# The seventh of nine token groups takes its second product from seven products of quarters; the weight sums move earlier and wholly to GpSimd

## The chip, the cores and the metric

One core of one Trainium2 chip runs the kernel. The metric is the device time of one execution in microseconds (us). Engines: TensorE (PE, matmuls; PEld its weight loads), VectorE (DVE), ScalarE (ACT), GpSimd (POOL), SyncE (SP, whose queue issues most DMAs).

## The reference

Windowed causal attention for 8 batches, 8 heads, 576 positions, head size 64, and behind it an MLP with SiLU for the 4608 rows of 512 that it gives:

```python
scores = scale * np.matmul(q, k.transpose(0, 1, 3, 2))
mask = (rel >= 0) & (rel < window)                 # window 128
scores = np.where(mask, scores + bias[None], -1000000000.0)
attn = np.exp(scores - np.max(scores, axis=-1, keepdims=True))
attn = attn / (np.sum(attn, axis=-1, keepdims=True) + 1e-09)
attn_out = np.matmul(attn, v).astype(np.float32)   # -> x, 4608 x 512
h = x @ w_in                                       # w_in 512 x 2048
g = h * (1.0 / (1.0 + np.exp(-h)))
return (g @ w_out).astype(np.float32)              # w_out 2048 x 512
```

## The kernel before

**Tiles and stages.** The 4608 rows are nine groups of 512, g = 0 to 8. For a group the 2048 columns of w_in are 16 blocks f; n = 16g + f counts them all. From group 2 on each float32 operand is a pair of float16 numbers, high part and remainder, and a product is three matmuls: high x high, high x remainder, remainder x high. `gemm1` makes h for one n in PSUM, `act1` takes tanh on ACT, `act2` makes h(1 + tanh) on DVE, `act3` rounds to `gh` on ACT, `act4` takes the remainder `gl` on DVE, and `gemm2` multiplies by w_out into four PSUM banks w, x, y, z, which collect over the group; `store` empties them.

**Groups in FAST** (7 and 8) do this otherwise. In them an n is a pair (t, j): 256 of the group's rows and two f blocks, j and j + 8, which makes a product of 2 x 2 quarters. `act_sums` forms sums of the quarters of g, so `act3` and `act4` work on seven blocks of 128 columns, and `gemm2_fast` uses 7 products of quarters (M1 to M7) where 8 would be plain: 21 matmuls of 256 columns. `join_products` and `add_corners` bring them together behind the last j of each t. The sums of w_out's quarters that this needs are made once, on POOL and ACT (`sum_float`, `sum_make`, `sum_hi`, `sum_lo`, for j = 0 to 7), and kept in SBUF. Group 8 (SEVEN) also makes h from 7 products; the sums of w_in for it (`in_float` to `in_lo`) are made in groups 2 to 4, stored to DRAM (`in_away`) and read back (`in_back`).

**Attention** is 72 pairs p (a tile of 128 rows, four of the heads). For each: `scores` on PE into the two PSUM banks "a" (L495), `row_max` on DVE (L526), `exps` on ACT, `p_hi` on ACT (L551), the remainder `p_lo` on POOL from pair 18 on (L557, helper line), two transposing DMAs on SP (`hl`, L567), `attend` on PE (`av`, L609), `normalize`, `x_hi`, `x_lo`. `lo16` (L443) and `v_lo` (L476) are remainders on DVE. The bank for `av` is again one of "a". `vscale_finish` makes a batch's scales, its last stage by a small matmul (L325) into a bank "a".

**What sets the order.** Nothing is scheduled by the machine: a table `plan` says at which position each function is issued, and every engine takes its instructions in the order of issue. A group has 64 positions, four for an n: two halves of `gemm1`, two of `gemm2`. Group 6 is 384 to 447. Pair p has its scores at `at(p)`, nine pairs to a group, 7 positions apart, in groups 1 to 6. `gemm2` of an n stands behind `gemm1` of a later one: one later in groups 0 to 6 (with none left over at a group's end), three later in group 7 (LAG), four in group 8.

```python
SUMS, SUMS_STEP = 302, 17
IN_SUMS = (186, 200, 214, 228, 242, 256, 270, 284)
FAST = (NG - 2, NG - 1)
left = LAG + (n >= SEVEN * NF - 1) if g in FAST else 1
```

## Time and profile before

| | |
|---|---|
| median of 3 runs | 901.03 us (900.76 to 901.49) |
| the profiled execution | 901.33 us |
| its span, first to last instruction | 899.5 us |
| busy: PE, PEld | 891.8 us (99%), 592.2 us (66%) |
| busy: DVE, ACT, POOL | 611.3, 613.3, 411.5 us |

The profile is of one execution. Its span leaves out some 1.8 us that lie around the instructions. Busy times add up over the whole span; what an engine's work is worth must be read from the stretch in which it lies. PE's sequence through a group is best seen in the chain of waits, which merges equal matmuls that follow each other.

### The profile page before, as it was taken

Reading aid. Unit: us, or ns where it says so; the run is one execution under the profiler, and the core shown is the slowest. Engines: PE = TensorE matmul, PEld = TensorE weight load, DVE = VectorE, ACT = ScalarE, POOL = GpSimd, SP = SyncE. Lnnn points to the kernel's source line nnn. Section 1 sums busy time; section 2 is a strip of 40 time slices with the busy share of each in tenths; the row PEclk is TensorE's granted clock in tenths of the full one; section 3 lists DMA queues with packets and bytes.
Section 4 is the critical chain, followed back from the end, with each engine's and each line's share of the span. In section 5 each row is a group of like instructions: output and inputs, shape, how many; then the busy total and the mean of one; then the engine's idle time right before and its main releaser. Section 6 shows DMA issues by size and latency. Waiting matters only on the chain. (4 is left out here: it accounts for less than half of the span.)

```text
span 899.5 us, 20129 instructions
## 1 busy us (share of the span) xinstructions
PE 891.8 (99%) x7657; PEld 592.2 (66%) x7657; DVE 611.3 (68%) x1591; ACT 613.3 (68%) x1336; POOL 411.5 (46%) x462
## 2 busy tenths in 40 slices
...
GB/s 301 402 204 230 274 56 134 71 94 95 106 205 224 204 95 89 228 175 212 142 176 118 129 106 147 89 96 81 135 145 85 60 107 162 85 37 7 20 26 24
DMA packets 206160, 120.98 MB, mean 134 GB/s; under 512 B 170864, under 2 KB 173040, under 8 KB 206064
## 3 DMA queue, kind: packets, MB, share of 16 engines
...
## 5 line engine op out<-in xcount | busy, mean ns | idle before, releaser
L1130 PE MATMUL o<-w,gh 128*128 128x512 f16 (+1 forms) x896 | 273.6, 387 | 0.1
L920 PE MATMUL h<-xt,w 128*128 128x512 f16 (+1 forms) x1344 | 269.7, 349 | 0.0
L557 POOL TENSOR_TENSOR hr<-t,hr 128x512 f16<-128x512 f32 (+1 forms) x108 | 119.7, 1121 | 253.3 <-ACT hr L551 170.7
L920 PEld LDWEIGHTS <-w 128*128 128x128 f16 x1344 | 126.3, 98 | 112.3 <-issue 3.3
L961 DVE SCALAR_TENSOR_TENSOR h<-gt,h 128x512 f32<-128x512 f32 x112 | 77.8, 694 | 159.9 <-ACT gt L955 159.6
L1130 PE MATMUL o<-w,gl 128*128 128x512 f16 (+1 forms) x448 | 172.0, 384 | 0.2
L955 ACT ACTIVATE gt<-h,tsc 128x512 f32<-128x512 f32 x112 | 76.3, 681 | 92.9 <-PE h L920 79.5
L1130 PEld LDWEIGHTS <-gh 128*128 128x128 f16 x640 | 59.3, 98 | 66.7
L526 DVE CUSTOM_DVE_ANT_0 t<-sp,tab 128x256 f32<-128x256 f32 (+1 forms) x288 | 99.9, 401 | 1.9 <-PE sp L502 1.3
L551 ACT ACTIVATE hr<-t 128x512 f16<-128x512 f32 (+1 forms) x128 | 74.1, 598 | 2.6 <-DMA hl<-hr 2.6
L541 ACT ACTIVATE t<-t,mx,vsc 128x256 f32<-128x256 f32 (+1 forms) x144 | 74.8, 578 | 1.2
L1007 DVE SCALAR_TENSOR_TENSOR gl<-h,gh 128x512 f16<-128x512 f32 x80 | 55.0, 687 | 24.2 <-ACT gh L993 23.8
L541 ACT ACTIVATE t<-t,mx 128x256 f32<-128x256 f32 (+1 forms) x144 | 61.8, 488 | 4.5 <-DVE mx L526 3.8
L993 ACT ACTIVATE gh<-h 128x512 f16<-128x512 f32 x80 | 47.2, 590 | 22.4 <-DVE h L961 22.1
L609 PEld LDWEIGHTS <-hl 128*128 128x128 f16 x1464 | 52.0, 98 | 15.8 <-issue 4.5
L171 POOL TENSOR_TENSOR x<-xs,x 128x256 f16<-128x256 f32 x54 | 39.1, 725 | 43.5 <-ACT x L648 43.3
L609 PE MATMUL av<-v,hl 128*128 128x65 f16 (+1 forms) x1464 | 55.4, 193 | 0.9 <-DVE mx L526 0.6
L1130 PEld LDWEIGHTS <-gl 128*128 128x128 f16 x320 | 31.3, 98 | 37.9 <-DVE gl L1007 0.3
L1130 PEld LDWEIGHTS o<-w,gh 128*128 128x128 f32 x256 | 45.6, 188 | 10.0 <-issue 0.5
L925 PE MATMUL h<-xh,w 128*128 128x512 f32 x128 | 44.5, 404 | 0.0
L892 PE MATMUL h<-xt,w 128*128 128x256 f16 x384 | 44.2, 273 | 0.0
L171 POOL TENSOR_TENSOR w<-wm,w 128x512 fp32r<-128x512 f32 x32 | 43.0, 1343 | 2.6
...
## 6 DMA issues: line engine op xcount, KB each, us to landing
...
```

The source lines that it names most:

```text
L171: engine.tensor_sub(out, a, b)
L526: nc.vector.tensor_tensor_reduce(out=st[p]["t"][u][:, h, 2 * P - n :], in0=st[p]["sp"][h][:, u, o].rearrange("p o c -> p (o c)"), in1=tab[ ...
L541: nc.scalar.activation(x, x, AF.Exp, bias=mx[:, 2 * u + h : 2 * u + h + 1], scale=scale)
L551: nc.scalar.activation(split_of(p, u, hr)[:, 0], t[:, :, 2 * P - n :], AF.Copy, scale=scale)
L557: nc.gpsimd.tensor_sub(hr[:, 1], t[:, :, 2 * P - n :], hr[:, 0])
L609: nc.tensor.matmul(av[:, 2 * u + h, : rhs.shape[-1]], lhs, rhs, start=(n == 0), stop=(n == len(seq) - 1), skip_group_check=True,)
L920: nc.tensor.matmul(o, w[:, wp, cc], x, start=start and k == 0, stop=stop, skip_group_check=True)
L955: nc.scalar.activation(gt, hps[n], AF.Tanh, scale=scale)
L961: nc.vector.scalar_tensor_tensor(out=h, in0=gt, scalar=1.0, in1=h, op0=ALU.add, op1=ALU.mult)
L993: nc.scalar.activation(gh, gt, AF.Copy, scale=cut_of(n))
L1007: nc.vector.scalar_tensor_tensor(out=gl, in0=gt, scalar=cut_of(n), in1=f32(gh) if n // NF < OUT16 else gh, op0=ALU.mult, op1=ALU.subtract)
L1130: nc.tensor.matmul(ops[ti], a[:, t], w, start=(f == 0 and i == 0), stop=(f == NF - 1 and i == len(seq) - 1), skip_group_check=True,)
```

## The change

Group 6 joins FAST: `gemm1` there runs by `gemm1_fast` (24 matmuls of 256 columns for 12 of 512), `gemm2` from seven products. Its `act_sums` run on POOL; group 7's (ALONE) stay on DVE. Since attention still runs in group 6, its products use banks w, x, y, z for both t. The lag grows from one to three within group 5 (`lag_of`), and the boundary from 5 to 6 and from 6 to 7 no longer works its n off to the end.

The sums of w_out are needed a group earlier: they start at position 178 (before 302) and take turns with those of w_in, 24 positions to a j for both. The copies that ACT made for them go to POOL (`copy_hi`), and w_in's quarters are formed in place. `away` is stored 7 positions behind the start of a w_in sum. Of each pair's two `p_lo`, that of u = 1 goes from POOL to DVE (LOW_DVE). The last batch's scales are finished at 268, 274, 281, 288, and several offsets of attention move by one to three positions.

```diff
--- before.py
+++ after.py
@@ -63,7 +63,7 @@
 OWN = ("w1_12", "w1_13")
 OWN_FIRST = ("w0_15", "w0_14")
 FREE = ("w1_14", "w0_15", "w0_14", "w1_12", "w0_13")
-FINISH = {1: (37, 42, 45), 2: (166, 168, 169, 170), 3: (268, 271, 273, 275)}
+FINISH = {1: (37, 42, 45), 2: (166, 168, 169, 170), 3: (268, 274, 281, 288)}
 BOUNDS = {2: (125, 4), 3: (195, 6)}
 LOAD1, REDUCE1 = (-9, -8, -6, -5, -4), (25, 21, 17, 13, 11)
 RAW16 = ("w1_0", "w1_1")
@@ -71,19 +71,37 @@
 PACKED = ("w1_4", "w1_5", "w1_6")
 LESS = 2
 CUT = 2.0 ** (LESS - 20)
-IN_TAGS = {0: "w1_2", 1: "w1_3", 2: "w1_0", 4: "w1_5"}
-IN_SUMS = (186, 200, 214, 228, 242, 256, 270, 284)
-IN_BACK = {2: 440, 3: 444, 4: 460, 5: 468, 6: 474, 7: 480}
-AWAY = ("w1_7", "w1_8")
+IN_TAGS = {0: ("w1_2", 1), 1: ("w1_3", 1), 2: ("w1_0", 1), 3: ("q", 2), 4: ("w1_5", 1), 5: ("x", 4), 6: ("x", 4)}
+SUMS, SUMS_STEP = 178, 24
+IN_GAP = 17
+HI_SUM, HI_IN = 1, 1
+IN_SUMS = tuple(SUMS + SUMS_STEP * j + IN_GAP for j in range(8))
+IN_AWAY = 7
+IN_BACK = {2: 462, 3: 484, 4: 470, 5: 490, 6: 494, 7: 480}
 X_TAGS = ("w1_1", "w1_4")
-X_SUMS = (450, 453, 456, 459, 462, 465, 468, 472, 471, 476, 474, 478, 479, 487, 481, 489)
+X_SHIFT = 4
+ALONE_POOL = 0
+ALONE_LATE = 6
+X_SUMS = tuple(X_SHIFT + n for n in (450, 453, 456, 459, 462, 465, 468, 472, 471, 476, 474, 478, 479, 487, 481, 489))
 NB = 2
-FAST = (NG - 2, NG - 1)
+FAST = (NG - 3, NG - 2, NG - 1)
+ALONE = NG - 2
 SEVEN = NG - 1
 HALF_F = NF // 2
 LAG = 3
-SUMS, SUMS_STEP = 302, 17
-OUT_TAGS = {3: ("w1_14", "w1_9"), 4: ("w1_13", "w1_14"), 6: ("w1_5", "w1_6")}
+RAMP = (4, 9)
+ACT_LATE = 6
+ACT_LOW = 2
+V_HI, V_LO = 8, 4
+IN_HI16, IN_LO16 = (9, 8), (6, 4)
+ATTEND = 11
+EXPS = (2, 3)
+P_HI = (3, 3)
+P_LO = (4, 5)
+X_OFF = 2
+LOW_DVE = 1
+X_DVE = 0
+OUT_TAGS = {3: ("q", 2), 4: ("q", 2), 5: ("q", 2)}
 SUM_TAGS = tuple(f"w1_{k}" for k in range(7, 15))
 MORE_TAGS = (("w1_15", 1), ("k", KSLOTS), ("k", KSLOTS))
 STATS, CONV_IN, CONV_OUT = 68, 55, 108
...
         hr = split_of(p, u, st[p]["hr", u])
         if p >= LOW_POOL:
-            nc.gpsimd.tensor_sub(hr[:, 1], t[:, :, 2 * P - n :], hr[:, 0])
+            minus(nc.vector if u and LOW_DVE else nc.gpsimd, hr[:, 1], t[:, :, 2 * P - n :], hr[:, 0])
             return
         nc.vector.scalar_tensor_tensor(
             out=hr[:, 1], in0=t[:, :, 2 * P - n :], scalar=PSCALE, in1=hr[:, 0], op0=ALU.mult, op1=ALU.subtract
...
             cols = slice(q * 4 * D, (q + 1) * 4 * D)
-            minus(nc.gpsimd if p >= LOW_POOL else nc.vector, xt[i][:, 1, cols], st[p]["x"], xt[i][:, 0, cols])
+            minus(nc.gpsimd if p >= LOW_POOL and not X_DVE else nc.vector, xt[i][:, 1, cols], st[p]["x"], xt[i][:, 0, cols])
             if q == 1:
...
 
+    def copy_hi(on_pool, out16, a):
+        if on_pool:
+            nc.gpsimd.tensor_copy(out16, a)
+        else:
+            nc.scalar.copy(out16, a)
+
     def sum_hi(j, k):
...
-        piece["q"] = [both[1][:, s].rearrange("p (s c) -> p s c", s=2) for s in range(2)]
-        w = pool.tile([P, 2, 4, DM // 2], F16, tag=IN_TAGS[j] if j < 2 else AWAY[j % 2], bufs=1, name=f"wx{j}")
+    def in_tile(j):
+        tag, bufs = IN_TAGS[j] if j < 2 else ("big", 2)
+        w = pool.tile([P, 2, 4, DM // 2], F16, tag=tag, bufs=bufs, name=f"wx{j}")
         win[j] = [w[:, part] for part in range(2)]
 
...
     def in_float(j, k):
         if k == 0:
-            in_pieces(j)
+            piece["room"] = pool.tile([P, 2, DM], F32, tag="big", name=f"wb{j}")
+        piece[k] = piece["room"][:, k]
+        r = piece[k]
         w = w16[0, j + k * HALF_F]
-        nc.gpsimd.tensor_add(piece["r"][k].rearrange("p (c f) -> p c f", c=NCC), w[:, 0], w[:, 1])
+        nc.gpsimd.tensor_add(r.rearrange("p (c f) -> p c f", c=NCC), w[:, 0], w[:, 1])
...
     def in_make(j, k):
-        (a11, a12), (a21, a22) = ([r[:, h * DM // 2 : (h + 1) * DM // 2] for h in range(2)] for r in piece["r"])
-        one, two = piece["q"]
+        (a11, a12), (a21, a22) = ([piece[k][:, h * DM // 2 : (h + 1) * DM // 2] for h in range(2)] for k in range(2))
         if k == 0:
-            nc.gpsimd.tensor_add(one[:, 0], a21, a22)
-            nc.gpsimd.tensor_sub(one[:, 1], one[:, 0], a11)
-        else:
-            nc.gpsimd.tensor_sub(two[:, 0], a11, a21)
-            nc.gpsimd.tensor_sub(two[:, 1], a12, one[:, 1])
+            nc.gpsimd.tensor_add(a22, a21, a22)
+            nc.gpsimd.tensor_sub(a21, a11, a21)
+        else:
+            nc.gpsimd.tensor_sub(a11, a22, a11)
+            nc.gpsimd.tensor_sub(a12, a12, a11)
...
     IN_WORK = (
-        [(in_float, 0)], [(in_float, 1)], [(in_make, 0)], [], [(in_make, 1)], [], [(in_hi, 0)], [(in_lo, 0)],
-        [(in_hi, 1)], [(in_lo, 1)],
+        [(in_float, 0)], [(in_float, 1)], [(in_make, 0)], [(in_make, 1), (in_hi, 1)], [(in_lo, 1), (in_hi, 0)], [],
+        [(in_lo, 0)],
     )
...
     def act_sums(n):
         if n == LAST:
             return
-        engine, a = nc.gpsimd if n // NF == SEVEN else nc.vector, gact[n]
+        engine, a = nc.vector if n // NF == ALONE and n % NF >= ALONE_POOL else nc.gpsimd, gact[n]
         pairs = a[:, 0:4].rearrange("p (a b) c -> p a b c", b=2)
...
         dt = F32R if n // NF < OUT16 else F16
-        gh = pool.tile([P, TG], dt, tag="gh", name=f"gh{n}")
-        gl = pool.tile([P, TG], dt, tag="gl", name=f"gl{n}")
+        if n // NF < OUT16:
+            gh, gl = (pool.tile([P, TG], dt, tag=tag, name=f"{tag}{n}") for tag in ("gh", "gl"))
+        else:
+            both = pool.tile([P, 2, TG], dt, tag=("gh", "gl")[n % 2], name=f"gb{n}")
+            gh, gl = both[:, 0], both[:, 1]
         if n // NF < IN16:
             (nc.vector.tensor_copy if at_edge(n) else nc.scalar.copy)(gh, gt)
         elif n // NF < OUT16 and at_edge(n):
...
         products, first = (M5, M2, M1, M3, M4, M7, M6), 4
-        if j == 0 and g == SEVEN:
+        if j == 0 and g != ALONE:
             first = 3
         elif j == 0 and t:
             products = (M3, M4, M5, M2, M1, M7, M6)
...
                 if j == 0 and side == 0 and a is gh:
-                    ops[b] = psum.tile([P, DM], F32, tag=("axaz" if t or g == SEVEN else "wxyz")[b], bufs=2 if (t or g == SEVEN) and b % 2 == 0 else 1, name=f"m{g}_{t}_{b}")
+                    free = g == SEVEN or g == ALONE and t
+                    tag = ("axaz" if free else "wxyz")[b]
+                    ops[b] = psum.tile([P, DM], F32, tag=tag, bufs=2 if tag == "a" else 1, name=f"m{g}_{t}_{b}")
                 for part in parts:
                     nc.tensor.matmul(
                         product(k), a[:, k], sum_part(k, j, part),
...
         if half == 0:
-            both = pool.tile([P, 2, 2, DM // 2], F32, tag="w1_6", bufs=1, name=f"of{g}_{t}")
-            st["out"] = [both[:, k] for k in range(2)]
-            st["once"] = once = pool.tile([P, 2, DM // 2], F32, tag="rv", bufs=2, name=f"once{g}_{t}")
-            nc.scalar.activation(once.rearrange("p a c -> p (a c)"), ops[1], AF.Copy, scale=scale)
+            if g < ALONE:
+                st["out"] = [pool.tile([P, 2, DM // 2], F32, tag="q", bufs=2, name=f"of{g}_{t}_{k}") for k in range(2)]
+            else:
+                both = pool.tile([P, 2, 2, DM // 2], F32, tag="w1_6", bufs=1, name=f"of{g}_{t}")
+                st["out"] = [both[:, k] for k in range(2)]
+            once = st["out"][1]
+            nc.scalar.activation(once, ops[1].rearrange("p (a c) -> p a c", a=2), AF.Copy, scale=scale)
             for k in range(2):
                 nc.vector.scalar_tensor_tensor(
                     out=st["out"][0][:, k], in0=product(M1), scalar=scale, in1=once[:, k], op0=ALU.mult, op1=ALU.subtract
                 )
             return
-        (corner, other), once = st["out"], st["once"]
+        corner, other = st["out"]
         nc.vector.scalar_tensor_tensor(
-            out=other, in0=ops[0].rearrange("p (a c) -> p a c", a=2), scalar=scale, in1=once, op0=ALU.mult, op1=ALU.add
+            out=other, in0=ops[0].rearrange("p (a c) -> p a c", a=2), scalar=scale, in1=other, op0=ALU.mult, op1=ALU.add
         )
...
     def store(g, ti):
         tag, bufs = ("x", 4) if ti > 1 else ("io", 2)
         if ti > 1 and g > 2:
-            tag, bufs = (OUT_TAGS[g][ti % 2], 1) if g in OUT_TAGS else ("big", 2)
+            tag, bufs = OUT_TAGS[g]
         ot = pool.tile([P, DM], F32, tag=tag, bufs=bufs, name=f"ot{g}_{ti}")
...
     SUM_WORK = (
-        [(sum_float, 0)], [(sum_float, 1)], [(sum_make, 0)], [(sum_make, 1)], [(sum_make, 2), (sum_hi, 0)],
-        [(sum_hi, 1), (sum_lo, 0)], [(sum_hi, 2)], [(sum_lo, 1)], [(sum_lo, 2)],
+        [(sum_float, 0)], [], [(sum_float, 1)], [], [(sum_make, 0)], [], [(sum_make, 1), (sum_hi, 0)], [],
+        [(sum_make, 2), (sum_hi, 1)], [(sum_lo, 0), (sum_hi, 2)], [], [(sum_lo, 1)], [], [(sum_lo, 2)],
     )
...
         put(n + 1, row_max, p, 1)
-        put(2 if p == 2 * GT else n + 2, exps, p, 0)
-        put(2 if p == 2 * GT else n + 3, exps, p, 1)
+        plain = p < LOW_POOL
+        put(2 if p == 2 * GT else n + (2 if plain else EXPS[0]), exps, p, 0)
+        put(2 if p == 2 * GT else n + (3 if plain else EXPS[1]), exps, p, 1)
...
+        elif not plain:
+            for u in range(2):
+                put(n + P_HI[u], p_hi, p, u)
+                put(n + P_LO[u], p_lo, p, u)
+                put(n + P_LO[u], p_transpose, p, u)
...
-                put(a - (7 if i < 2 * GT else 5), v_hi, i)
-                put(a - (3 if i == 2 * GT else 4), v_lo, i)
+                put(a - (7 if i < 2 * GT else V_HI), v_hi, i)
+                put(a - (3 if i == 2 * GT else 4 if i < 2 * GT else V_LO), v_lo, i)
...
         if j > 1:
-            put(IN_SUMS[j] + 17, in_away, j)
+            put(IN_SUMS[j] + IN_AWAY, in_away, j)
             put(IN_BACK[j], in_back, j)
...
+        def lag_of(n):
+            g, f = divmod(n, NF)
+            if n == NG * NF - 1 or f == NF - 1 and g + 1 < FAST[0]:
+                return 0
+            if g in FAST:
+                return LAG + (n >= SEVEN * NF - 1)
+            return 1 + (f >= RAMP[0]) + (f >= RAMP[1]) if g + 1 in FAST else 1
...
-                left = LAG + (n >= SEVEN * NF - 1) if g in FAST else 1
-                if f == NF - 1 and (g not in FAST or g == NG - 1):
-                    left = 0
+                left = lag_of(n)
...
+                        if n % NF == NF - 1 and g not in FAST and g + 1 not in FAST:
                             turn_over(n)
                         else:
-                            late = 1 if n == 0 else 9 if n == SEVEN * NF - 1 else 11 if n == SEVEN * NF - 2 else 4 if g in FAST and n % NF > 1 else 2
-                            ahead(late + 1 + (late == 4) if n % NF else late, act4, n)
+                            late = 1 if n == 0 else 9 if n == SEVEN * NF - 1 else 11 if n == SEVEN * NF - 2 else ALONE_LATE if g in FAST and n % NF > 1 else 2
+                            if g in FAST and g < ALONE:
+                                late = ACT_LATE
+                            ahead(late + (ACT_LOW if g in FAST and g < ALONE else 1) + (late == ALONE_LATE and g >= ALONE) if n % NF or g in FAST else late, act4, n)
                             ahead(late, act3, n)
                             if not edge:
                                 ahead(1, act2, n)
                 else:
```

Three places in the engines' orders. First PE, the second product of n = 100 in group 6; `o` are the output banks, `m` the products, `w16_1` is w_out, `ws` and `wt` are its sums. Before:

```order
L1130 LDWEIGHTS gh100_9389
L1130 MATMUL o6_0_9106<-w16_1_2_3504,gh100_9389 128x512
L1130 LDWEIGHTS gh100_9389
L1130 MATMUL o6_0_9106<-w16_1_2_3504,gh100_9389 128x512
L1130 LDWEIGHTS gl100_9390
L1130 MATMUL o6_0_9106<-w16_1_2_3504,gl100_9390 128x512
L1130 LDWEIGHTS gh100_9389
L1130 MATMUL o6_1_9110<-w16_1_2_3504,gh100_9389 128x512
```

Now:

```order
L920 MATMUL h103_9607<-xt24_7685,w16_0_3_2486 128x256
L1069 LDWEIGHTS gh100_9479
L1069 MATMUL m6_0_1_9228<-w16_1_6_4238,gh100_9479 128x256
L1069 LDWEIGHTS gh100_9479
L1069 MATMUL m6_0_1_9228<-w16_1_6_4238,gh100_9479 128x256
L1069 LDWEIGHTS gh100_9479
L1069 MATMUL m6_0_1_9228<-w16_1_2_3504,gh100_9479 128x256
L1069 LDWEIGHTS gh100_9479
L1069 MATMUL m6_0_1_9228<-w16_1_2_3504,gh100_9479 128x256
L1069 LDWEIGHTS gh100_9479
L1069 MATMUL m6_0_3_9233<-ws4_6814,gh100_9479 128x256
```

Before there are 12 such matmuls of 512 columns for an n; now 21 of 256, each with its own weight load.

Second DVE, in group 4, ahead of the small matmul of batch 3's scales (`row3` holds them; `sp` are scores, ISA is `row_max`). Before:

```order
L317 TENSOR_SCALAR row3_6607<-row3_6607 1x1
L318 TENSOR_TENSOR row3_6607<-row3_6607 1x1
L319 TENSOR_SCALAR row3_6607<-row3_6607 1x3
L320 TENSOR_SCALAR row3_6607<-row3_6607 1x3
L321 TENSOR_SCALAR row3_6607<-row3_6607 1x1
L322 TENSOR_TENSOR row3_6607<-row3_6607 1x1
L515 MEMSET sp47_0_6626 128x2x64
L515 MEMSET sp47_1_6627 128x2x64
L526 ISA t47_0_6673,mx47_6652<-sp47_0_6626,tab_67 128x256
```

Now the row maxima of pair 49, which stand ahead of that matmul:

```order
L989 SCALAR_TENSOR_TENSOR h71_6850<-gt71_6894,h71_6850 128x512
L191 SCALAR_TENSOR_TENSOR hr48_1_6845<-t48_1_6806,hr48_1_6845 128x512
L1038 SCALAR_TENSOR_TENSOR gb71_6912<-h71_6850,gb71_6912 128x512
L494 SCALAR_TENSOR_TENSOR v2_70<-rv24_6810,vsc2_4453,v1_69 128x512
L544 ISA t49_0_6961,mx49_6952<-sp49_0_6926,tab_67 128x256
L544 ISA mx49_6952 128x1
```

The scale arithmetic now stands behind pair 48's maxima, a pair earlier; ahead of these maxima there are `act2` and `act4` of n = 71, the remainder of pair 48 (L191, `hr48_1`) and `v_lo`.

Third DVE in group 6, around the row maxima. Before:

```order
L1007 SCALAR_TENSOR_TENSOR gl99_9286<-h99_9255,gh99_9285 128x512
L961 SCALAR_TENSOR_TENSOR h100_9334<-gt100_9349,h100_9334 128x512
L476 SCALAR_TENSOR_TENSOR v2_70<-rv32_9252,vsc3_6705,v1_69 128x512
L515 MEMSET sp65_0_9355 128x2x64
L515 MEMSET sp65_1_9356 128x2x64
L526 ISA t65_0_9394,mx65_9381<-sp65_0_9355,tab_67 128x256
L526 ISA mx65_9381 128x1
```

Now (`io97` is `act4` of n = 97, in two pieces):

```order
L1031 SCALAR_TENSOR_TENSOR io97_9135<-gt97_9022,gt97_9134 128x640
L1031 SCALAR_TENSOR_TENSOR io97_9135<-gt97_9022,gt97_9134 128x256
L191 SCALAR_TENSOR_TENSOR hr63_1_9142<-t63_1_9096,hr63_1_9142 128x512
L992 SCALAR_TENSOR_TENSOR gt99_9222<-gt99_9222,h99_9187 128x512
L533 MEMSET sp64_0_9246 128x2x64
L533 MEMSET sp64_1_9247 128x2x64
L544 ISA t64_0_9289,mx64_9272<-sp64_0_9246,tab_67 128x256
```

`act4` has 640 and 256 columns for 512, and the remainder `hr63_1` of the pair before has come in ahead of `act2`.

## Rows read from the trace of the kernel before

**Rows 1.** The page, busy time: engine, us, share, instructions.

```profile
PE 891.8 (99%) x7657; PEld 592.2 (66%) x7657; DVE 611.3 (68%) x1591; ACT 613.3 (68%) x1336; POOL 411.5 (46%) x462
```

**Rows 2.** View by stretches, groups 6 and 7.

```profile
core 0: us, PE busy (x) PEld busy (x) DVE busy (x) ACT busy (x) POOL busy (x), PEclk, DMA share, GB/s
644.00:742.00 98.00, 98.00 (x822) 49.84 (x821) 54.94 (x159) 64.95 (x128) 57.35 (x63) 1.00 0.46 109
742.00:813.00 71.00, 71.00 (x676) 63.78 (x675) 53.30 (x113) 28.80 (x51) 2.55 (x4) 1.00 0.35 90
```

**Rows 3.** Chain of waits, 640 to 760 us: start us, us, engine, tile, line, count.

```profile
641.12 0.72 PE av L609 x24
641.84 2.59 PE o L1130 x12
644.43 2.59 PE h L920 x12
647.02 0.78 PE sp L495 x24
647.79 2.70 PE h L920 x12
...
693.18 2.59 PE o L1130 x12
...
750.36 2.62 PE h L892 x24
752.98 2.29 PE m L1036 x21
```

**Rows 4.** Timeline, 474 to 480 us: start us, us, engine, line, tiles, [idle <-releaser].

```profile
477.30 0.56 DVE L322 TENSOR_TENSOR row<-row 1x1 f32<-1x1 f32 x1
...
478.78 0.07 DVE L526 DVE_READ_ACCUMULATOR2_ANT mx<- 128x1 f32 x1
...
479.00 0.35 PE L325 MATMUL vs<-row,ones 1*128 1x8 f32 x2 [0.82 <-DVE mx L526]
```

**Rows 5.** Three lines of DVE by themselves: durations ns least/median/most.

```profile
L1007 DVE SCALAR_TENSOR_TENSOR gl<-h,gh x80: 672/690/693, 256.6 to 738.0; 128x512 f16<-128x512 f32 x80
...
L443 DVE SCALAR_TENSOR_TENSOR packed<-r,vsc,packed x36: 731/746/1669, 349.8 to 716.3; 128x512 f16<-128x512 f32 x36
...
L559 DVE SCALAR_TENSOR_TENSOR hr<-t,hr x20: 669/681/1342, 48.0 to 150.0; 128x512 f16<-128x512 f32 x20
```

**Rows 6.** Lines by shape, DVE, 742 to 813 us: busy us, mean ns.

```profile
L1000 DVE SCALAR_TENSOR_TENSOR gl<-gt,gh 128x640 f16<-128x640 f32 x7 | 5.7, 818 | 0.2 <-ACT gh L983 0.2
...
L1000 DVE SCALAR_TENSOR_TENSOR gl<-gt,gh 128x256 f16<-128x256 f32 x7 | 2.9, 417 | 0.0
```

**Rows 7.** Lines by shape, whole span, DVE: group 7's joins.

```profile
L1101 DVE SCALAR_TENSOR_TENSOR of<-m,gsc,once 128x512 f32<-128x512 f32 x4 | 3.0, 742 | 0.0
...
L1079 DVE SCALAR_TENSOR_TENSOR of<-m,gsc,of 128x256 f32<-128x256 f32 x8 | 3.5, 474 | 0.0
```

**Rows 8.** Lines by shape, whole span, POOL: two inputs of 512 and 256 columns.

```profile
L557 POOL TENSOR_TENSOR hr<-t,hr 128x512 f16<-128x512 f32 x96 | 111.5, 1174 | 218.9 <-ACT hr L551 141.3 <-issue 76.8 <-POOL hr L557 0.5
...
L713 POOL TENSOR_TENSOR wq<-wr 128x256 f32<-128x256 f32 x8 | 5.8, 726 | 0.0
```

**Rows 9.** Timeline, 690 to 712 us, columns as in group 4.

```profile
690.01 0.69 DVE L961 SCALAR_TENSOR_TENSOR h<-gt,h 128x512 f32<-128x512 f32 x1 [3.32 <-ACT gt L955]
...
691.37 0.69 DVE L1007 SCALAR_TENSOR_TENSOR gl<-h,gh 128x512 f16<-128x512 f32 x1 [0.66 <-ACT gh L993]
...
694.15 0.08 DVE L526 DVE_READ_ACCUMULATOR2_ANT mx<- 128x1 f32 x1
...
695.61 0.89 PE L609 MATMUL av<-v,hl 128*128 128x65 f16 x24
...
699.67 2.64 SPq L567 DMA_TRANSPOSE hl<-hr  x2
...
706.28 0.89 PE L609 MATMUL av<-v,hl 128*128 128x65 f16 x24
```

**Rows 10.** DMA issues: count, median us from issue to landing.

```profile
hl<-hr SPq DMA_TRANSPOSE x128, 2.8
```

50 lines of the change are left out of this document (26 added, 24 removed).

## The prediction, made before the change was run

> **What bounds the kernel now.** I read the page first: TensorE (PE) is busy 891.8 us, 99% of the span [rows 1]. The share alone proves little, so I looked at the stage that the change rewrites, group g = 6, about 644 to 742 us, in the view by stretches: PE 98.00 of 98.00 us at granted clock 1.00 (2.4 GHz), against ACT 64.95, POOL 57.35 and DVE 54.94 [rows 2]. The chain of waits there is PE rows laid end to end with nothing between them [rows 3]. So PE's own work sets the pace, and the other engines matter only where they make PE wait. The one such wait of note behind the start is 0.82 us at 479.00 [rows 4].
>
> **The main term: 24 products of 512 columns become 45 of 256.** For each f block, groups 2 to 6 run 12 matmuls of 512 columns for h (2.59 us) and 12 for the output (2.59 us), 5.18 us together [rows 3]. A group in FAST runs 24 of 256 columns (2.62 us) and 21 of 256 (2.29 us), 4.91 us [rows 3]; these are rows of group 7, which does this already, as group 6 now will. That is 0.27 us less for each f, and 16 x 0.27 = **4.32 us** for group 6. Twice the instructions for h cost 0.03 us in the 2.62, so they are counted. All of it lies on PE's path. Attention stays: 9 pairs of 0.78 + 0.72 us [rows 3], the extra 0.1 us of the matmuls behind a score block too.
>
> **The second term: the wait at 479.00.** PE's small matmul of the third batch's scales (L325) waits for DVE, and starts 0.15 us behind the end of the second row-maximum of a pair [rows 4]: it needs one of the two PSUM banks "a" that hold that pair's scores. The row maxima were late because the scale arithmetic, whose last instruction starts at 477.30 [rows 4], and the two memsets stood ahead of them on DVE; the order shows this. FINISH moves that arithmetic behind another pair's maxima, and the matmul behind the next pair's scores and 12 matmuls of h. Bounds: nothing is won if DVE is as late there, and all of 0.82 us if it isn't. Ahead of those maxima DVE will have an act4 (0.69), the new remainder (0.68) and a v_lo. I put them at 5.3 to 6.3 us behind the end of the h before (an estimate from these durations); PE comes there after 2.59 + 0.78 + 2.70 = 6.07 us. So I take **0.8 us**.
>
> **What the new work costs beside PE, group 6.** DVE: the nine remainders `p_lo` of u = 1 come from POOL, 9 x 0.68 = 6.1 us (20 of that kind ran on DVE early on: median 681, at most 1342 ns [rows 5]). act4 becomes 640 + 256 columns, 0.818 + 0.417 us [rows 6] for 0.690 [rows 5], 16 x 0.545 = 8.7 us. The joins at the end of the first half take 2 x 0.742 + 4 x 0.474 = 3.4 us [rows 7]. So 54.9 + 6.1 + 8.7 + 3.4 = **73 us** of the 92 that PE will need (16 x 4.91 + 9 x 1.50). It has cover. ACT: act3 goes from 512 to 896 columns; ACT had 33 us free and loses the group's copies for the sums. Nothing. POOL: each f adds three additions of at most 0.73 us [rows 8], 35 us in all, but loses the sums of w_out (they end at position 360, group 6 starts at 384) and half of `p_lo`. Nothing.
>
> **POOL in groups 3 to 5.** A round of 24 positions (24 x 98/64 = 36.8 us by group 6's stretch [rows 2] and its 64 positions) now has one w_out sum and one w_in sum. Eight two-input instructions of 512 columns at 1.17 us, ten of 256 at 0.73 and six copies, which the trace doesn't show in this form; they cost over nothing and at most what a two-input form of 512 columns costs, 1.17. I take the middle, 0.6. That is 9.4 + 7.3 + 3.6 = 20.3 us, with 10.6 us for copies at the upper bound 23.7 (all this 1.17 and 0.73 from [rows 8]). Attention leaves POOL 1.17 us of `p_lo`, 0.73 of `x_lo` and about 0.4 of `v_hi` per pair, 3.4 pairs, 7.8 us. 28 of 36.8 us, at most 32: POOL keeps up. ACT is rid of these copies.
>
> **Edits that I cost at nothing.** The stores to "away" stay 12 x 256 KB on SP's queue, now 7 positions behind the start of a sum instead of 17; what is queued behind them there are transposes and loads. The reads back move to 462 to 494 with group 8 starting at 512, some 18 positions of over 1.2 us ahead of the first use of the latest. X_SUMS goes back by 4 positions of the same group 7, which has DVE 53.3 of 71 us busy [rows 2]. hi16, lo16, v_hi and both p_hi move by one to three positions, 1.5 to 5 us on ACT, DVE and POOL, all into stretches with room. Stores of groups 3 to 5 change their buffers only. RAMP lets the lag grow in group 5, so that group 6 starts with one h block (2.62 us) between the last output product of group 5 and its own first; three stood there at the edge from 6 to 7. The four banks are emptied two by two, by ACT and DVE in turn, each some 0.74 us (as [rows 7]), the first two of them half a product earlier. That is covered.
>
> **Where the new waits come from.** (a) Group 6 keeps banks w, x, y, z in both halves, since attention holds "a", and group 7 begins with them. At the middle and the end of group 6 the join has to empty w before the fourth product of what follows: 0.742 + 2 x 0.474 = 1.7 us on DVE, under one h block (2.62) and three products (0.65 at least). Cost: nothing unless DVE is 1.5 us behind; then what exceeds it. (b) An attend (av) needs a bank "a", free once the second maximum of the next pair's scores is done. At 694.15 + 0.08 us that read ends, and av starts at 695.61: 1.4 us of room [rows 9]. The maxima stood behind an act2 for which DVE had waited 3.32 us [rows 9], so ACT is what makes them late. In the new group 6 scores and av lie 4.9 us apart (2.62 + 2.29) where they lay 5.2 (2 x 2.59), and DVE has 0.68 to 1.34 us more in its queue. So the room is between +0.4 and -0.5 us in the late pairs, about half of the nine. I put **0.5 us** for both.
>
> **The sum.** The profiled execution took 901.33 us, 0.30 above the median. 901.33 - 4.32 - 0.82 + 0.5 = 896.7; less the 0.30, **896.4 us**.
>
> **Rivals.**
> *The gain is partly given back at the banks (0.18).* As in (b), but with DVE 0.5 to 0.9 us too late in four pairs and again at one join: 2 to 3.5 us instead of 0.5, so 897.9 to 899.4. For it: those late maxima. Against: `p_lo` is issued some three positions ahead of them, and PE waited for no such av in group 6 before.
> *POOL in groups 3 to 5 holds up the transposes (0.06).* SP issues the pair's two transposes in 2.64 us from 699.67, and av starts at 706.28 [rows 9]; landing takes 2.8 us in the median [rows 10], which leaves 1.2 us. If in each of the 8 rounds the new quarter sums wait for the store that frees their buffer, and u = 0's remainder behind them is 1.8 us late, that costs 8 x 0.6 = 4.8 us: about 900.7, no change. Against: two floats (2.3 us) cover most of the store.
> *It gets slower: DVE's remainder blocks the activation chain where the lag is still 1 (0.05).* Place: groups 1 to 5, 45 pairs. There `p_lo` now sits on DVE between act2 and act4, or ahead of both, and it waits for ACT's copy. act4 ends at 691.37 + 0.69 = 692.06 and its product starts at 693.18 [rows 3, 9]: 1.12 us of room. At its longest (1.34) it overruns this by 0.2 us, 45 x 0.2 = 9.9 us: 901.0 - 5.1 + 9.9 = 905.8. It is slower from 0.15 us of overrun per pair on. Against: the median is 0.68, and other alignments of pairs and f blocks leave more.
> *It gets slower: DVE and POOL shut each other out, and DVE bounds group 6 (0.03).* With one input in PSUM, `gl` took 672 to 693 ns in all 80 cases; `lo16`, the same shape with both in SBUF, took 731 to 1669, median 746 [rows 5]. Group 6 gets 41 more of the second kind (9 `p_lo`, 32 of act4, whose first input moves from PSUM to SBUF). If each took 0.92 us longer, DVE would need 73 + 38 = 111 us for 92: 901.0 - 5.1 + 18.9 = 914.8. It decides from (92 - 73)/41 = 0.46 us each. Against: the median is 15 ns above the least, with POOL busy over half of the time. The Trainium skill has this as a rule ("SBUF — State Buffer", section "Who interferes with whom"): a VectorE instruction with two SBUF inputs and a GpSimd one that reads SBUF share a read interface, and whoever is second fully blocks. By that rule the trace agrees in kind, 693 against 1669 ns at most; how often it strikes is what the medians decide.
>
> That the products aren't fewer is ruled out by the order: PE has 21 rows of 256 columns for an f of group 6.
>
> **How the numbers follow.** A change under 0.2% (1.8 us) can't be told from none here. The forecast, 895.5 to 897.8, has 0.66; the give-back 0.18, of which 0.03 lies above 899.2; POOL 0.06; the two slower ones 0.05 and 0.03; 0.02 is left for something unseen on the slow side, such as a longer tail. Faster by over 0.2%: 0.66 + 0.15 + 0.02 of the POOL case if half as bad = 0.83. Within: 0.03 + 0.04 + 0.01 = 0.08. Slower: 0.09. The low end is every gain without a stall (901.03 - 5.14 = 895.9) less half a us for the 0.7 us over which the runs spread: 895.4. The high end takes in the give-back, 899.6. What is left out is 0.15.
>
> **What would show it.** Right: in the profile after, group 6 has h rows of x24 and 2.62 us and m rows of x21 and 2.29 us, is some 4.3 us shorter, and the small scale matmul has no wait. PE's busy time falls by some 4.3 us to 887.5, and group 7 and 8 keep their lengths. Wrong: waits of PE for DVE maxima at av or at the banks w to z in group 6 (first rival), of av for hl in groups 3 to 5 (second), of the output products for gl in groups 1 to 5 (third), or DVE over nine tenths busy in group 6 with act4 far above 0.82 us (fourth).

## The result, and the profile after

| | median us | range, runs | ratio to before, interval |
|---|---|---|---|
| kernel before, beside it | 900.93 | 900.45 to 901.55, 6 | |
| changed kernel | 908.21 | 906.60 to 910.34, 6 | 1.0081 [1.0066, 1.0095] |

The kernel became slower by 7.3 us; the prediction said 4.6 faster. The profiled execution took 908.87 us, with a span of 907.1 against 899.5. The page's busy line, the counterpart of [rows 1]:

```profile
PE 890.3 (98%) x7993; PEld 626.1 (69%) x7993; DVE 667.9 (74%) x1672; ACT 597.1 (66%) x1304; POOL 436.0 (48%) x504
```

PE did less work, 890.3 us for 891.8, and yet ended later, so it waited. The waits of PE in the changed kernel (who waited for whom: us in total, times, longest):

```profile
PE av L627 <- DMA hl<-hr: 8.8, 7, 1.8
...
PE av L627 <- DVE mx L544: 0.7, 1, 0.7
```

The same view of the kernel before:

```profile
...
PE vs L325 <- DVE mx L526: 0.8, 1, 0.8
PE av L609 <- DVE mx L526: 0.6, 1, 0.6
PE av L609 <- DMA hl<-hr: 0.2, 1, 0.2
```

So av now waits seven times for hl, the transposes of a pair's probabilities, 8.8 us in all. The seven stand at 374.15 (0.90 us), 408.43 (1.85), 421.01 (1.73), 575.60 (1.73), 693.76 (1.07), 725.70 (0.82) and 736.66 (0.68). The one wait for maxima lies far ahead of group 6, at 66.26; the kernel before has its own at 65.81. The view by stretches, groups 3 to 6, shows where PE lost its 98 or 99 us; changed kernel, then before (for group 6 of before see [rows 2]):

```profile
core 0: us, PE busy (x) PEld busy (x) DVE busy (x) ACT busy (x) POOL busy (x), PEclk, DMA share, GB/s
348.00:446.00 98.00, 92.96 (x733) 46.35 (x732) 56.56 (x150) 70.95 (x162) 71.55 (x82) 1.00 0.61 165
446.00:545.00 99.00, 98.63 (x824) 49.93 (x823) 69.83 (x185) 60.63 (x119) 80.28 (x88) 1.00 0.52 126
545.00:644.00 99.00, 97.20 (x790) 48.50 (x790) 67.26 (x166) 59.79 (x120) 72.21 (x81) 1.00 0.53 114
644.00:742.00 98.00, 95.37 (x1142) 80.23 (x1137) 77.31 (x186) 64.74 (x129) 61.35 (x70) 1.00 0.51 112
```

```profile
348.00:446.00 98.00, 97.99 (x787) 49.09 (x786) 58.54 (x155) 78.79 (x181) 63.10 (x68) 1.00 0.76 189
446.00:545.00 99.00, 98.18 (x828) 49.92 (x825) 61.51 (x175) 65.03 (x127) 61.96 (x66) 1.00 0.54 123
545.00:644.00 99.00, 98.82 (x797) 49.53 (x794) 58.18 (x156) 66.44 (x137) 63.86 (x72) 1.00 0.46 105
```

No engine beside PE is over 82% busy in any of these groups, so none of them is late by the sum of its work there. Group 6 itself has the predicted rows, as [rows 3] had them for group 7 (chain of waits, 673 to 694 us):

```profile
673.79 2.62 PE h L920 x24
...
682.93 2.29 PE m L1069 x21
...
690.99 2.72 DMA hl<-hr
...
693.76 0.54 PE av L627 x12
```

**One lost wait, followed back.** Timeline of the changed kernel, group 5 (start, duration, engine, line, tiles, [idle before <- releaser]):

```profile
561.14 3.05 SPq L698 DMA_TRANSPOSE xt<-x  x2
...
563.49 0.71 ACT L569 ACTIVATE hr<-t 128x256 f16<-128x256 f32 x2
564.29 2.13 SPq L783 DMA_DIRECT2D away<-wx  x2
564.68 0.41 DVE L191 SCALAR_TENSOR_TENSOR hr<-t,hr 128x256 f16<-128x256 f32 x1
566.47 0.42 SPq L480 DMA_DIRECT2D rv<-v  x1
569.82 0.70 POOL L488 TENSOR_SCALAR v<-rv,vsc 128x512 f16<-128x512 f32 x1 [6.08 <-DMA rv<-v]
570.47 0.67 POOL L189 TENSOR_TENSOR hr<-t,hr 128x256 f16<-128x256 f32 x1
570.55 1.14 DVE L494 SCALAR_TENSOR_TENSOR v<-rv,vsc,v 128x512 f16<-128x512 f32 x1 [2.67 <-POOL v L488]
571.17 2.50 SPq L585 DMA_TRANSPOSE hl<-hr  x2
...
575.60 0.36 PE L627 MATMUL av<-v,hl 128*128 128x65 f16 x6 [1.73 <-DMA hl<-hr]
```

ACT's high half was done at 564.2 and DVE's remainder at 565.1. GpSimd's remainder started at 570.47, behind `v_hi` (L488), for which GpSimd stood 6.08 us: the load rv had been issued only at 566.47, behind two transposes and the two stores to "away" on SP's queue. So both transposes left at 571.17 and av found them 1.73 us too late. DVE too stood, 2.67 us, at `v_lo`. The same pair in the kernel before:

```profile
559.37 2.93 SPq L567 DMA_TRANSPOSE hl<-hr  x2
560.42 0.67 POOL L557 TENSOR_TENSOR hr<-t,hr 128x256 f16<-128x256 f32 x1
562.92 0.70 POOL L470 TENSOR_SCALAR v<-rv,vsc 128x512 f16<-128x512 f32 x1 [1.21 <-DMA rv<-v]
```

There the remainder went ahead of `v_hi`. The wait at 374.15 has the same form: rv was issued at 362.01, `v_hi` started at 366.07 and the remainder at 368.22, though ACT's high half was done at 363.8. At 408.43 the lateness reaches av by a longer way (timeline of the changed kernel):

```profile
386.73 0.70 POOL L488 TENSOR_SCALAR v<-rv,vsc 128x512 f16<-128x512 f32 x1 [1.44 <-DMA rv<-v]
...
391.38 2.64 SPq L585 DMA_TRANSPOSE hl<-hr  x2
...
394.07 0.57 SPq L242 DMA_DIRECT2D vm<-v  x1
...
397.11 0.63 ACT L256 ACTIVATE vm<-vm 128x512 f32<-128x512 f32 x1 [1.02 <-DMA vm<-v]
...
402.67 1.24 SPq L585 DMA_TRANSPOSE hl<-hr  x1
```

A late `v_hi` makes the remainder and both transposes of one pair late, the load vm stands behind these on SP's queue, ACT stands 1.02 us for vm, and so the next pair's high halves and transposes come late. Before the wait at 421.01 `v_hi` stood only 0.94 us for rv, and this wait stays when that load is moved (second set).

The change puts `v_hi` three positions earlier (V_HI 8 for 5), which is in front of the remainder and two positions behind its own load. Over the whole span the idle time of GpSimd put down to rv rises from 1.8 us to 57.0 in 17 waits.

### The profile page after: what moved, and what is told of

It is laid out like the page before. It is cut to its first block, busy times and chain, and to the rows that moved or that the text cites. A ratio compares the mean times of both kernels' runs of the same rounds, so it can differ in the third digit from the quotient of the medians.

```text
span 907.1 us, 20908 instructions
## 1 busy us (share of the span) xinstructions
PE 890.3 (98%) x7993; PEld 626.1 (69%) x7993; DVE 667.9 (74%) x1672; ACT 597.1 (66%) x1304; POOL 436.0 (48%) x504
## 4 chain that ended last, share of the span: by engine, by line
PE 73%; DVE 6%; ACT 5%; DMA 4%; POOL 2%; issue 2%; SPq 1%; DVEq 0%; POOLq 0%; ACTq 0%
PE o L1166 21%; PE h L948 18%; PE m L1069 10%; PE h L920 8%; PE av L627 4%; PE h L953 3%; PE sp L520 3%; PE h L891 2%; DMA hl<-hr 2%; PE sp L513 2%; PE hb L891 2%; DVE t L544 1%; ACT t L559 1%; DMA rv<-v 1%; DVE h L989 1%
## 5 line engine op out<-in xcount | busy, mean ns | idle before, releaser
L948 PE MATMUL h<-xt,w 128*128 128x512 f16 (+1 forms) x1152 | 224.2, 344 | 0.0
L1166 PE MATMUL o<-w,gb 128*128 128x512 f16 x768 | 179.5, 379 | 0.4 <-DVE gb L1038 0.4
L948 PEld LDWEIGHTS <-w 128*128 128x128 f16 x1152 | 108.5, 98 | 91.7 <-issue 3.3
L1166 PEld LDWEIGHTS <-gb 128*128 128x128 f16 x768 | 72.3, 98 | 83.6 <-DVE gb L1038 1.1
L189 POOL TENSOR_TENSOR hr<-t,hr 128x512 f16<-128x512 f32 (+1 forms) x54 | 62.3, 1154 | 111.9 <-ACT hr L569 55.3
L920 PE MATMUL h<-xt,w 128*128 128x256 f16 x768 | 89.8, 273 | 0.0
L1166 PE MATMUL o<-w,gh 128*128 128x512 f32 x256 | 83.1, 405 | 0.5 <-ACT gh L1020 0.5
L920 PEld LDWEIGHTS <-w 128*128 128x128 f16 x768 | 74.1, 98 | 9.1
L488 POOL TENSOR_SCALAR v<-rv,vsc 128x512 f16<-128x512 f32 x30 | 23.9, 797 | 72.1 <-DMA rv<-v 57.0
L1024 ACT ACTIVATE gb<-h 128x512 f16<-128x512 f32 x64 | 37.8, 590 | 25.3 <-DVE h L989 25.2
L1038 DVE SCALAR_TENSOR_TENSOR gb<-h,gb 128x512 f16<-128x512 f32 x64 | 43.9, 686 | 12.0 <-ACT gb L1024 11.6
L1166 PE MATMUL o<-w,gl 128*128 128x512 f32 x128 | 50.7, 396 | 0.2
```

The lines of the kernel that those rows point to most:

```text
L189: engine.tensor_sub(out, a, b)
L920: nc.tensor.matmul(out, w[:, wp, cc], xt[g, "g"][:, 2 * t : 2 * t + 2, xp * NCC + cc], start=half == 0 and i == 0, stop=i == len(seq) - 1, ...
L948: nc.tensor.matmul(o, w[:, wp, cc], x, start=start and k == 0, stop=stop, skip_group_check=True)
L1038: nc.vector.scalar_tensor_tensor(out=gl, in0=gt, scalar=cut_of(n), in1=f32(gh) if n // NF < OUT16 else gh, op0=ALU.mult, op1=ALU.subtract)
L1166: nc.tensor.matmul(ops[ti], a[:, t], w, start=(f == 0 and i == 0), stop=(f == NF - 1 and i == len(seq) - 1), skip_group_check=True,)
```

## The experiments

Theory A was that this wait of `v_hi` is the cause. Times are medians; the kernel before ran beside each set (901.77, 901.41, 901.07, 900.92 and 901.75 us in the five sets). The sets are compared by their ratios.

### First set: the parts of the change taken back one by one

`e1_vhi5`, late `v_hi` again:
```diff
-V_HI, V_LO = 8, 4
+V_HI, V_LO = 5, 4
```


> V_HI back from 8 to 5, nothing else. Theory A (GpSimd stands at v_hi until the load of v has landed, which is issued only two positions earlier, and p_lo and DVE's v_lo stand behind it): GpSimd's 57 us of waits for rv fall below 10, TensorE's waits for hl in groups 3 to 5 (6.2 us in four cases) go, and the time falls by 4 to 7 us to 901 to 904. Rival B (GpSimd's queue is too full of sums and copies): less than 1.5 us changes. Rival C (DVE's new remainder is what comes late): less than 1 us changes.

Measured: 913.79 us, ratio 1.0136 [1.0119, 1.0153], slower than the change. GpSimd's wait for rv went and group 3 was busy 97.15 of 98 us, but new waits came in groups 4 and 6 (PE's waits):

```profile
PE av L627 <- DMA hl<-hr: 6.3, 9, 1.3
PE vt L321 <- DVE mx L544: 2.4, 1, 2.4
```

So theory A in its first form fell: taking `v_hi`'s move back alone made the kernel slower still, so the move isn't a loss by itself. In the new order `v_hi` stands at its old place behind sums and a copy (L811 to L815 and L748, before 478.03). DVE's `v_lo` then stood 22.3 us in 12 waits for it (2.7 us in one in the changed kernel), at 478.76 with the row maxima behind it, for which PE's vt stood 2.4 us. The old place together with the earlier load was not run.

`e2_plo_pool`, both remainders on GpSimd:
```diff
-LOW_DVE = 1
+LOW_DVE = 0
```


> LOW_DVE = 0: both remainders of a pair on GpSimd as before, the rest as in the change. Rival C (the remainder on DVE blocks activations and maxima): 3 us faster or more. Theory A: no gain; GpSimd has 1.17 us more per pair behind the same wait, so slower by 0 to 6 us. Rival B: clearly slower, over 5 us, since 1.17 us per pair are 54 x 1.17 = 63 us more on GpSimd.

Measured: 909.91 us, 1.0087 [1.0072, 1.0102], av's waits for hl 7.4 us in 8. DVE's half of the remainder is not the cause; GpSimd's wait was still 51.7 us.

`e4_copies_act`, the sums' copies back on ScalarE:
```diff
-HI_SUM, HI_IN = 1, 1
+HI_SUM, HI_IN = 0, 0
```


> HI_SUM = HI_IN = 0: the copies of the sums go back to ACT, the rest as in the change. Rival B (GpSimd too full): GpSimd loses some 20 us of copies in groups 2 to 5, TensorE's waits for hl there fall by more than half, 3 us faster or more. Theory A: within 2 us of the change, since the waits for the load stay.

Measured: 917.90 us, 1.0176 [1.0158, 1.0194], neither of the two answers. Less work on GpSimd, and worse: output products now wait 4.2 us for ACT's gb. At the longest of these waits (2.36 us, at 581.00) ACT had stood 5.58 us at a copy (L750) for GpSimd's sum, with gb behind it. The copies' move to GpSimd is a gain.

`e5_six_plain`, group 6 in the old form:
```diff
-FAST = (NG - 3, NG - 2, NG - 1)
+FAST = (NG - 2, NG - 1)
-OUT_TAGS = {3: ("q", 2), 4: ("q", 2), 5: ("q", 2)}
+OUT_TAGS = {3: ("q", 2), 4: ("q", 2), 5: ("q", 2), 6: ("rv", 2)}
```


> FAST without group 6: its products are plain again, with the sums, the copies, the remainder on DVE and the offsets as in the change (and the growing lag in group 6 instead of 5). What group 6 itself brings is then read alone: the columns are worth 4.3 us and its stalls in the change cost 2.6, so theory A expects 1 to 4.3 us slower than the change, 909 to 912.5. If the new form of group 6 is what makes the change slow, it comes out faster than the change by 2 us or more.

Measured: 911.96 us, 1.0108 [1.0091, 1.0126]. The loss lies ahead of group 6, in what was only moved.

### Second set: the load moved instead of its user

`e6_load_early`:
```diff
-                put(n + 1, load_v, i)
+                put(n + (1 if i < 2 * GT else -2), load_v, i)
```


> The changed kernel, with the load of a block's values issued three positions earlier (about 4.5 us), so that GpSimd's v_hi, kept at its early place, finds them landed. Theory A, second form (GpSimd stands at v_hi for a load that was issued two positions before, 57 us in 17 waits, and the remainder p_lo behind it sends the transposes late; putting v_hi late instead only made the same work late on GpSimd and VectorE): GpSimd's wait for rv falls from 57 us to under 10, the waits of av for hl in groups 3 and 5 (four of 0.9 to 1.85 us) go, and the time falls by 5 to 8 us, to 900 to 903. Rival B (GpSimd carries too much in groups 2 to 5 whether it waits or not: 72 to 80 us busy of 98): the waits move on and the time stays at 906 to 910. Rival E (the added loads in flight slow the transposes' own landing, 4 to 5 us in group 3 against a median of 2.8): av still waits for hl at 406 and 419, 907 to 911.

Measured: **903.00 us** (902.07 to 904.55, 9 runs), 1.0020 [1.0010, 1.0030], apart from the change's 1.0081: 5 us are back. The waits at 374, 408 and 576 are gone; the one at 421, here at 418 (1.67 us), and group 6's stay. The pair of the timeline above, in this kernel:

```profile
557.30 0.45 SPq L480 DMA_DIRECT2D rv<-v  x1
557.84 3.24 SPq L698 DMA_TRANSPOSE xt<-x  x2
...
561.17 1.86 SPq L783 DMA_DIRECT2D away<-wx  x2
561.51 0.69 POOL L488 TENSOR_SCALAR v<-rv,vsc 128x512 f16<-128x512 f32 x1 [1.54 <-DMA rv<-v]
562.17 0.67 POOL L189 TENSOR_TENSOR hr<-t,hr 128x256 f16<-128x256 f32 x1
563.13 2.53 SPq L585 DMA_TRANSPOSE hl<-hr  x2
...
569.52 0.53 PE L627 MATMUL av<-v,hl 128*128 128x65 f16 x12
```

The load now stands ahead of xt and away; everything behind it is on time, and av waits for nothing. My expectation missed one number: GpSimd's idle time put down to rv fell only from 57.0 to 54.9 us. That total doesn't tell harmful from harmless: 57.0 and 54.9 us go with times that lie 5 us apart.

`e7_load_early_dve`, that and group 6's sums of the activations on DVE:
```diff
-        engine, a = nc.vector if n // NF == ALONE and n % NF >= ALONE_POOL else nc.gpsimd, gact[n]
+        engine, a = nc.gpsimd if n // NF == SEVEN else nc.vector, gact[n]
```


> As the run before, and group 6's sums of the activations on VectorE in place of GpSimd, so that its p_lo has no three sums ahead of it. If group 6's remaining waits (1.07, 0.82 and 0.68 us for hl) come from these sums, the time is 2 to 3 us under the run before; if VectorE, 77 of 98 us busy there already, then becomes the engine that is late (gb, maxima), it is 0 to 6 us above it.

Measured: 910.89 us, 1.0102 [1.0080, 1.0124]. Scores now wait for DVE's normalisation (sp for xs 4.4 us in 2) and av for maxima (2.9 in 2). None of group 6's three waits for hl is left. That fits the sums on GpSimd as their cause, though PE's other waits also give the transposes more time. GpSimd is the better engine for these sums.

`e8_before_vhi8`, the kernel **before** with that one number:
```diff
-                put(a - (7 if i < 2 * GT else 5), v_hi, i)
+                put(a - (7 if i < 2 * GT else 8), v_hi, i)
```


> The kernel before with one edit of the change alone: v_hi three positions earlier (8 in place of 5 before av). Theory A: GpSimd waits for rv for 30 to 60 us in all, as in the changed kernel, and if that wait alone is the cause the time rises by 4 to 9 us, to 905 to 910. If the wait costs only beside the denser sums of the change (rival B), GpSimd has room to catch up and the time stays within 900 to 903.

Measured: 905.80 us, 1.0045 [1.0028, 1.0062]. Its waits of PE:

```profile
PE av L609 <- DMA hl<-hr: 4.0, 4, 2.2
```

The longest stand at 416.24 (2.16), 572.31 (0.89) and 647.37 (0.72). The first two are at av of the same pairs as the changed kernel's at 421.01 and 575.60, without any of the change's other parts. For them GpSimd stood 6.57 and 4.97 us at `v_hi` for rv, with the remainder behind it.

`e9_vhi_act`, e6 with `v_hi` on ScalarE:
```diff
-        if i <= GT:
+        if i <= GT or i >= 2 * GT:
```


> The changed kernel with the early load, and v_hi of the blocks from group 2 on by ScalarE in place of GpSimd: 24 or so copies of 1.2 us leave GpSimd, about 0.6 us each come to ScalarE. Rival B (GpSimd's own load is what makes p_lo late): 2 us or more under the first of these runs. Theory A (the wait, not the load): no more than 1 us away from it, or above it where ScalarE's chain gt to gb becomes late.

Measured: 905.38 us, 1.0041 [1.0026, 1.0055], no better than e6 with 26 us less work on GpSimd. av's waits for hl stay (4.8 us in 6, in e6 4.6 in 5), so nothing here speaks for GpSimd's amount of work (rival B); what the copies cost on ScalarE is in the time too.

### Third set: the remainders one position earlier

In e6, a stretch of group 6's trace reads like the changed kernel's, here:

```profile
685.06 0.72 POOL L1001 TENSOR_TENSOR gt<-gt 128x256 f32<-128x256 f32 x1 [3.66 <-DVE r L645]
685.75 1.18 POOL L1002 TENSOR_TENSOR gt<-gt 128x256 f32<-128x256 f32 x1
687.00 0.92 POOL L1003 TENSOR_TENSOR gt<-gt 128x128 f32<-128x128 f32 x1
687.88 1.33 POOL L189 TENSOR_TENSOR hr<-t,hr 128x512 f16<-128x512 f32 x1
...
689.24 3.28 SPq L585 DMA_TRANSPOSE hl<-hr  x2
...
693.76 0.54 PE L627 MATMUL av<-v,hl 128*128 128x65 f16 x12 [1.07 <-DMA hl<-hr]
```

The remainder stands behind three sums, which came late from DVE. Three of these four instructions also ran long: 1.18, 0.92 and 1.33 us, where the shortest of their kind in group 6 took 0.73, 0.45 and 1.15. That is 1.1 us, as much as the wait. Beside them `act4` ran on DVE, from 686.26, and took 1.94 us for both pieces (1.24 in [rows 6]). Whether the place behind the sums or this lengthening makes the wait, no run separates.

I queued the remainder earlier: `e10_load_plo` is e6 with
```diff
-P_LO = (4, 5)
+P_LO = (3, 4)
```


> The changed kernel with the early load (run e6_load_early, 903.0 us) and the remainder p_lo queued one position earlier on both engines, so that on GpSimd it stands ahead of group 6's sums of the activations, which waited for VectorE until 679.15 and held it back from 677.8 to 681.96. Theory A (what is left is p_lo standing behind other work in GpSimd's queue): the waits for hl at 418, 688, 720 and 731 (1.67, 0.86, 0.81, 0.68 us, 4.0 in all) go and the time falls by 3 to 4 us, to 899 to 900, under the kernel before. Rival B (GpSimd carries too much): p_lo is on time, the sums behind it become late, PE waits for the sums gt or gmore in group 6, and the time stays at 902 to 904.

`e11_load_plo33` is the same with `P_LO = (3, 3)`:

> As the run before with both halves' remainders at the same position as their high halves (3 and 3 in place of 3 and 4): VectorE's half then comes ahead of a product's gb and of the maxima. Theory A: within 1 us of the run before, the waits for hl having gone already; if VectorE's own queue is what is late at the end of group 6 (1.0 us wait for maxima at av), it is 1 to 4 us above.

`e12_load_plo_six` is e10 with e5's two edits:

> As the first of these three runs, but group 6 in the old form (both products in full, the lag no longer growing there). This prices the prediction's main term with the cover restored: 16 x 0.27 = 4.3 us above the first run, if group 6 then gives all that its shorter products promise; 0 to 2 above it, if its sums and additions cost as much as they save.

Measured: 933.40 us, 1.0367 [1.0339, 1.0394]; 963.80, 1.0701 [1.0673, 1.0729]; 929.07, 1.0305 [1.0288, 1.0321]. The largest misses of the study: I had moved DVE's half as well. It now stands in front of work for which PE waits, until ACT has made the high half (waits in e10):

```profile
DVE hr L191 <- ACT hr L569: 51.5, 36, 2.6
...
PE sp L513 <- DVE xs L656: 10.8, 12, 2.2
```

Since the waits run through all groups, e12 says nothing clean on group 6. In the expectations of e11 and e17 a wait of 1.0 us for maxima is put into group 6; it stands at 66.22 us, far ahead of it.

### Fourth and fifth set: GpSimd's half alone, and the other sides of the slot

`e13_plo_gp_early` is e6 with `P_LO = (3, 5)`; `e14_plo_gp_six` has it from group 6 on alone:
```diff
-                put(n + P_LO[u], p_lo, p, u)
-                put(n + P_LO[u], p_transpose, p, u)
+                first = n + (3 if u == 0 and n >= 6 * SLICE * NF - 8 else P_LO[u])
+                put(first, p_lo, p, u)
+                put(first, p_transpose, p, u)
```


> The changed kernel with the early load, and of the remainders only GpSimd's half queued one position earlier, in all groups from 2 on; VectorE's half keeps its place, which run e10_load_plo moved too (there VectorE stood 51.5 us in 36 waits at p_lo for ScalarE's p_hi, and normalisations, maxima and products behind it were late). Theory A (the loss left in group 6 is p_lo behind the three sums on GpSimd; that of e10 was VectorE's half): group 6's waits for hl go, 899.5 to 901.5. Rival B (GpSimd too full, or SP held at the transposes, so that any earlier p_lo makes others late): 903 to 915.

> As the run before, but the earlier place only from group 6 on (position 376). Theory A: the three waits for hl in group 6 (0.86, 0.81 and 0.68 us, 2.35 in all) go, 900 to 901.5, and group 6's gain shows as 3 to 4 us against the kernel before. Rival B: other waits (sums gt, gmore, VectorE's maxima) take their place, 902.5 to 905.

Measured: 913.67 us, 1.0139 [1.0126, 1.0152], and 904.43, 1.0038 [1.0026, 1.0051]. Theory A for group 6 missed: in e13 av waits 8.6 us in 7 again, in e14 group 6's waits stand at other pairs (669, 690, 711).

`e15_plo_loads_later` is e14 and `e18_early_loads_later` e6 with batch 3's loads two positions later:
```diff
-BOUNDS = {2: (125, 4), 3: (195, 6)}
+BOUNDS = {2: (125, 4), 3: (197, 6)}
```


> As the run before, and batch 3's loads for its scales (vm, qs) two positions later, so that no 512 KB load is issued between the two transposes of a pair in group 3. Rival E (loads in flight slow the landing of hl: the last wait of 1.67 us at 418, whose transpose was issued 5.3 us earlier): that wait goes and the time is 1 to 2 us under the run before. Theory A (p_lo's lateness on GpSimd alone sets it): the wait stays, within 0.7 us.

> The changed kernel with the early load, and batch 3's loads for its scales two positions later, without the earlier remainders of e14 and e15 (whose difference was 1.6 us). Rival E: the wait at 418 goes and nothing takes its place, 901 to 902. If the slack at av is simply used up and the wait moves to another pair (in e15 it moved to 374): 902.5 to 903.5.

Measured: 902.88 us, 1.0018 [1.0008, 1.0027], and 903.28, 1.0012 [1.0003, 1.0021]; e18 can't be told from e6. In both the wait at 418 goes and one of 1.17 or 1.30 us comes at 373 to 375: moved, not removed. e15 is 1.6 us under e14, but their intervals touch.

`e16_before_vhi8_early` is e8 with e6's early load:

> The kernel before with v_hi three positions earlier (905.8 us with that edit alone) and the load of the values three positions earlier too. Theory A (v_hi's wait for its load is what costs, not its place): back to 900.5 to 902.5. If the early place of v_hi itself costs, by its turn on GpSimd ahead of p_lo: 904 to 906.

Measured: 903.85 us, 1.0033 [1.0020, 1.0046]: neither of the two answers. The 4.4 us of e8 become 2.9, and the intervals overlap, so the early load's gain isn't shown here by time. In the profiles the loss in group 3 falls from 3.8 to 0.7 us and that of group 5 from 1.1 to nothing, but a new wait of 1.46 stands at 644.

`e17_early_six_plain` is e6 with e5's two edits:

> The changed kernel with the early load (run e6, 903.0 us), and group 6 in the old form, both products in full. It prices the prediction's main term where groups 2 to 5 run nearly without waits. If group 6's shorter products bring what the prediction said less the waits seen in e6 (16 x 0.27 = 4.3 us, less three waits for hl of 2.35 and one for maxima of 1.0): about 1 us above e6, 903.5 to 904.5. If the gain is as large as between the changed kernel and run e5 (3.75 us): 906 to 908.

Measured: 906.53 us, 1.0055 [1.0039, 1.0070]. Group 6 in the old form runs without one wait (view by stretches):

```profile
644.00:742.00 98.00, 98.00 (x832) 50.84 (x831) 61.02 (x168) 60.80 (x118) 20.36 (x23) 1.00 0.48 107
```

`e19_early_av_later` is e6 with av one position later in group 6:
```diff
-            a = n + (15 if p < 4 * GT else 13 if p < 4 * GT + 2 else ATTEND + ((p - 4 * GT - 2) % EACH == EACH - 1))
+            a = n + (15 if p < 4 * GT else 13 if p < 4 * GT + 2 else ATTEND + (384 <= n < 448) + ((p - 4 * GT - 2) % EACH == EACH - 1))
```
(and the same term added to V_HI and V_LO, so that these stay).

> The changed kernel with the early load, and in group 6 alone av one position later (v_hi and v_lo stay where they are). Theory A for group 6 (the remainders, behind the sums on GpSimd, leave the transposes 0.7 to 0.9 us too late for an av that a position later would not wait): the three waits for hl go, 900 to 901.5. Rival (the slot is tight on both sides, since the next scores need the bank that av's normalisation frees): waits of sp for xs come instead, 903 to 908.

Measured: 908.06 us, 1.0067 [1.0053, 1.0082]. No wait for hl is left in group 6; in its place:

```profile
PE sp L513 <- DVE xs L656: 5.7, 6, 1.5
```

av's slot is tight on both sides: one position later, the next pair's scores wait for the bank that av's normalisation must free.

## Where the time went

How much later than in the kernel before the score blocks of the same pair start (PE's timelines; places by the time of before), as the growth in each stretch, us:

| stretch of before | changed | e6 | e17 | e8 |
|---|---|---|---|---|
| to 102 | +0.5 | +0.5 | +2.2 | -0.8 |
| 102 to 343 | +1.0 | +1.4 | +2.0 | +0.8 |
| 343 to 429 (group 3) | +5.6 | +1.6 | +1.8 | +3.8 |
| 429 to 561 (group 4 on) | -0.7 | -1.0 | -1.2 | +0.2 |
| 561 to 582 (group 5) | +2.2 | 0.0 | 0.0 | +1.1 |
| 582 to 647 | 0.0 | 0.0 | +0.4 | +0.9 |
| 647 to the end (group 6 on) | -0.9 | -0.9 | +0.3 | 0.0 |
| span against 899.5 | +7.6 | +1.7 | +5.5 | +6.1 |

Groups 3 and 5 made 7.8 of the 7.6 us; the early load takes 6.2 of these back. Group 6's shorter products bring 1.2 us (e6 against e17, -0.9 against +0.3), as does the pair e5 and the changed kernel; the medians' differences, 3.5 and 3.75 us, hold also what differs ahead of group 6, such as e17's +2.2 at the beginning and 3.9 us in e5 at 561 to 582.

## Why the prediction was wrong, step by step

- **The step that failed**: "hi16, lo16, v_hi and both p_hi move by one to three positions ... all into stretches with room", under the edits that I cost at nothing. I priced `v_hi` by its duration (0.70 us) and the room on GpSimd. I didn't ask what it waits for and what stands behind it. With its load left where it was, the move cost about 5 us: so much comes back when the load moves too (e6). On the kernel before the same move alone cost 4.4 us (e8), of which 2.9 stay with the load moved (e16, where the intervals overlap). Taking the move back alone is no cure (e1): what failed is the move without its load, and a price that had no wait in it. The trace shows the order kept to the letter: the remainder, whose inputs were there at 564.2, started at 570.47 behind `v_hi`. The Trainium skill ("Perfetto Trace Analysis", section "Tensor Engine Instruction (MATMUL, LD_WEIGHTS)") states that ACT, DVE and GpSimd are strict FIFOs; by that rule the trace agrees. The prediction's same paragraph named transposes and loads as queued behind the stores to "away" and went on without a price: on that queue rv stood behind them.
- **The main term** (4.32 us) was right in PE's columns: rows of x24 with 2.62 and x21 with 2.29 us. It was wrong as time: 0.9 us is measured (table). Three waits for hl in group 6 took back 2.57 us; no wait for maxima did. av's blocks between group 6's first and last scores are 0.5 us longer as well (7.6 us busy for 7.1). What makes the last 0.3 us is not shown. The step behind it is "each f adds three additions ... Nothing" for POOL: the total is right (POOL 61.35 of 98 us), but the sums stand ahead of the remainder in the queue. PE's busy time was to fall to 887.5 us and came to 890.3; the score blocks of the early groups, which are busy 41.9 us for 40.4, make half of that gap.
- **The second term** (0.8 us) came true: the small scale matmul (L343 now) waits for no DVE, and the changed kernel gains 0.7 us in group 4. The moved scale arithmetic (L326 to L328) stands ahead of a gb there, for which PE's output product stood 0.37 us at 488.00.
- **DVE in group 6, and the fourth rival**: 73 us were forecast, 77.31 of 98 measured, so DVE, 79% busy and not nine tenths, doesn't bound group 6. The rival's other sign is there: `act4` far above 0.82 us. By shape, 644 to 742 us:

```profile
L1031 DVE SCALAR_TENSOR_TENSOR gl<-gt,gh 128x640 f16<-128x640 f32 x8 | 9.5, 1185 | 0.0
...
L1002 POOL TENSOR_TENSOR gt<-gt 128x256 f32<-128x256 f32 x16 | 14.5, 905 | 0.0
```

The 640-column pieces of `act4` took 1185 ns in the mean for even n and 1043 for odd n (tile io), for 818 in group 7, where the sums run on DVE; GpSimd's additions took 905 for 726 [rows 8]. So the rival's mechanism, two engines that lengthen each other's instructions, fits group 6 as a part of its loss; no run isolates it.

- **POOL in groups 3 to 5**: 28 of 36.8 us, 76%, were forecast; 73%, 81% and 73% were measured (71.55 of 98, 80.28 and 72.21 of 99 us). The load was right (in its working the copies' upper bound is 7.0 us, 6 x 1.17, and not 10.6; the 23.7 is right), and neither e9 nor e4 gained by less work on GpSimd.
- **The second rival** (POOL holds up the transposes, 0.06) had the right waiter and releaser, av for hl in groups 3 to 5, with the wrong holder: not the sums waiting for a store but `v_hi` waiting for its load. It got 4.8 us, "no change"; groups 3 and 5 lost 7.8.
- **The first rival** expected group 6 to lose to the maxima at the banks. There was none: all three waits of group 6 are for hl.
- **The third rival**, DVE's remainder in front of the activation chain, didn't occur in the change: the only output product that waited for DVE's gb, 0.37 us, had scale arithmetic ahead of it. One position earlier (e10) DVE's remainder does stand in front of other work, at 30 us over e6, but there the scores wait for the normalisation; output products waited for gb in e11, 14.4 us in 4.

**Open.** Of the growth between 102 and 343 us PE's list shows a part: 0.5 us for ACT's gh at about 141, in the changed kernel, e6, e17, e8 and e16 alike and not in the kernel before, and 0.57 (e6) and 1.02 (e17) for hl at 274 and 276. Another 0.6 us in the changed kernel, e6 and e17 is a score block, at 219 in the changed kernel, that takes 1.78 us for 1.17 and has no wait in the list; in e9 the profile puts 0.50 us in this block down to DVE (L366). None of these was tested. What makes the last wait of group 3, at 418, is open too: it moves with batch 3's loads, but the time doesn't (e18 against e6). Why e16 stays above the kernel before, and what e1 would give with the earlier load, was not tried. No version beat the kernel before: the best, e15, e18 and e6, stand 0.1 to 0.2% above it.
